# Chunk attention and a feed-forward block on one core: q and k loaded as one 4 KB run per partition

## The chip, the cores and the metric

The kernel runs on one core of a Trainium2 chip. The metric is the device time in microseconds (us) of one execution. Three runs of the kernel before took 244.71, 244.99 and 245.13 us; the median is 244.99. A separate, profiled execution gives the trace that the numbers of this text come from.

The core has engines that run side by side: TensorE (PE, matmuls; its weight loads are listed as PEld), VectorE (DVE), ScalarE (ACT), GpSimd (POOL) and SyncE (SP). They share 16 DMA engines. A tile in on-chip memory has 128 partitions; "partitions x elements" says how much an instruction works on.

## The reference

There are 8 batches, 8 heads, 576 tokens and 64 elements per head. Attention is local: each chunk of 64 tokens attends to itself alone. The result, with the heads side by side, is the input of a feed-forward block without a nonlinearity.

```
scores = scale * matmul(q_c, k_c transposed)          # 64 x 64 per chunk and head
attn   = exp(scores - max) / (sum + 1e-9)
x      = matmul(attn, v_c), as 4608 tokens x 512
a, b   = x @ w1, x @ w2                               # 512 -> 1024
out    = ((a * b) @ w3) @ w_out                       # 1024 -> 1024 -> 512
```

All inputs and the output are float32. The kernel computes in bf16 with float32 sums.

## The kernel before, in words

**Blocks.** The 4608 tokens are 72 chunks, four to a block: p = 0 to 17 counts blocks of 256 tokens, and a group g is two blocks. 576 tokens are nine chunks, so six of the blocks (2, 4, 6, 11, 13, 15) reach over the end of a batch; `spans` (line 118) cuts their loads in two.

**The order is written out by hand.** The string ORDER at the head of the file is a list of steps such as `T3.0`: a letter for a function and its arguments. Each engine gets its instructions in the order of the string, and `inorder` keeps it. So a late instruction makes everything late that stands behind it on its engine. The steps that the prediction speaks of:

- `R0`, `R1` (line 134): load block 0 of q and of k as float32, on SP's queue and on ACT's. `K0`, `K1` (line 140): ACT casts them to bf16.
- `q`, `k` (line 148): load a later block of q or k on POOL's queue, which casts to bf16 under way. POOL issues all weight and v loads on the same queue, in the order of the string.
- `T p.s` (line 202): DVE transposes q (s = 0) or k (s = 1) of block p, tile qk to tile qkT. DVE's transpose works on squares of 32 partitions by 32 elements, in the order in which it reads.
- `G` (line 212), only for blocks from 8 on: SP moves qkT to qkm, a form with 64 partitions, by DMAs (line 200).
- `S` (line 221): PE computes the scores of a block, from qkT for the blocks up to 7 (two products over 32 elements), from qkm after that (one over 64).
- `E` (line 238): ACT takes the exponential. `P` (line 245): PE multiplies with v and, by a column of ones in the v tile, sums the rows. `N` (line 265): DVE takes the reciprocal and normalises. `X` (line 279): DVE transposes to the tile xt, for the later blocks by way of xm and moves (`H`).
- `A`, `B` (lines 328, 332): PE multiplies with w1 and w2, `C` (line 335): ACT copies the first, `M` (line 339): DVE multiplies the two to the tile ab. For groups 0 and 1 this is done per block, with 256 columns, later per group with 512.
- `V`, `W`, `Z` (lines 391 to 406): w3 and w_out are multiplied together once, on the chip. DVE transposes w3 (tile w3T, line 393), PE multiplies.
- `O`, `Y`, `Q` (lines 363 to 387): PE multiplies ab with that product, ACT copies, SP stores.
- `D` (line 304): multiplications of zeros. They fill PE's time ahead of the first steps, in a fixed number.

PSUM, where PE writes, has four tiles, which S, P, A with B, W and O take in turn (`psum`). A branch at the end (`do_rescue`) computes everything again in a safer way if a check of the sums fails; it isn't entered with these inputs, but it calls the same `load_qk` and `do_T`.

**Where q and k lie.** In a quadrant of 32 partitions there is one chunk. Before the change a partition holds two neighbouring tokens (t) of all eight heads (h): eight runs of 2 x 64 float32, 512 B each, are read from memory for it, and eight of 256 B are written as bf16. Partition y of the quadrant has tokens 2y and 2y + 1. The transpose reads a partition's 1024 elements in the order in which they lie: h, t, half of the head's 64 elements (e), 32 elements. It turns "32 partitions y by 32 elements" into "32 partitions by 32 values of y". In qkT a head has its 64 tokens side by side (`[P, 2, 2, 2, H, CH]`, the last index is the token), so the 32 values of y are written two elements apart.

Of the kernel before, what the change touches and what calls it, by code (L numbers as in the profile page):

```python
# [44 lines left out]
def kernel(  # L45
# [11 lines left out]
    nc = tc.nc  # L57
    B, H, S, D = q.shape
    P = 128
    BL = 32  # L60
    NB = P // BL
    CH = 64
# [14 lines left out]
    bf = mybir.dt.bfloat16  # L77
    f32 = mybir.dt.float32
# [4 lines left out]
    io = ctx.enter_context(tc.tile_pool(name="io", bufs=2))  # L83
    asb = ctx.enter_context(tc.tile_pool(name="asb", bufs=2))
    msb = ctx.enter_context(tc.tile_pool(name="msb", bufs=2))
    ps = ctx.enter_context(tc.tile_pool(name="ps", bufs=4, space=bass.MemoryType.PSUM))

    def inorder(ins):
        tc.keep_in_program_order(ins)
        return ins  # L90
# [4 lines left out]
    def load(dst, src):  # L95
        return inorder(nc.gpsimd.dma_start(dst, src))  # L96
# [21 lines left out]
    def spans(c0, n):  # L118

        at = 0  # L120
        while at < n:
            b, c = divmod(c0 + at, NCH)
            m = min(n - at, NCH - c)
            yield at, b, c, m
            at += m
# [2 lines left out]

    qk_t = {}

    HH = H // 2
    raw_t = {}

    def do_R(s):

        raw_t[s] = msb.tile([P, H, 2 * D], f32, tag="o_sb", name="raw")
        inorder((nc.sync, nc.scalar)[s].dma_start(
            raw_t[s][:], (q, k)[s][0, :, 0:4 * CH, :].rearrange("h (p t) d -> p h (t d)", t=2)))

    def do_K(s):  # L140
        if 0 not in qk_t:
            qk_t[0] = io.tile([P, 2, H, 2 * D], bf, tag="qk", bufs=5, name="qk")
        inorder(nc.scalar.copy(qk_t[0][:, s], raw_t[s][:]))  # L143

    def heads(h):
        return slice(0, H) if h is None else slice(h * HH, (h + 1) * HH)

    def load_qk(p, which, h=None):
        if p not in qk_t:
            qk_t[p] = io.tile([P, 2, H, 2 * D], bf, tag="qk", bufs=5, name="qk")  # L150
        for s in which:
            for at, b, c, m in spans(4 * p, 4):
                load(qk_t[p][at * BL:(at + m) * BL, s, heads(h)],
                     (q, k)[s][b, heads(h), c * CH:(c + m) * CH, :].rearrange("h (p t) d -> p h (t d)", t=2))

    def do_w(p):

# [36 lines left out]
    qkT_t, qkm_t, s_t, e_t, pv_t, xn_t, xm_t, xt_t = {}, {}, {}, {}, {}, {}, {}, {}  # L194
# [4 lines left out]
    def move(dst, src):  # L199
        inorder(nc.sync.dma_start(dst, src))  # L200

    def do_T(p, s, h=None):


        g = p // 2
        if g not in qkT_t:
            qkT_t[g] = asb.tile([P, 2, 2, 2, H, CH], bf, tag="qkT", bufs=2, name="qkT")
        inorder(nc.vector.transpose(  # L208
            qkT_t[g][:, :, p % 2, s, heads(h)].rearrange("p e h (y t) -> p h t e y", t=2),
            qk_t[p][:, s, heads(h)].rearrange("p h (t e y) -> p h t e y", t=2, e=2)))  # L210

    def do_G(g, a):

# [218 lines left out]
    def do_rescue():  # L432
# [8 lines left out]
        for g in range((NP + 1) // 2):  # L441
            for p in (2 * g, 2 * g + 1):
                load_qk(p, (0, 1))
                load_v(p)
                do_T(p, 0)
                do_T(p, 1)
                s_ps = psum("s_ps")
                for h in range(H):
# [36 lines left out]
            t.clear()  # L485
            t.update(was)

    def load_q(p, h=None):
        load_qk(p, (0,), h)

    def load_k(p, h=None):
        load_qk(p, (1,), h)

    def load_w12(i):
        n = DF // 4
# [3 lines left out]
    def load_half3(i):  # L499
# [8 lines left out]


    do = {"q": load_q, "k": load_k, "v": load_v, "i": load_w12, "o": load_wo, "h": load_half3, "T": do_T, "S": do_S, "R": do_R, "K": do_K, "E": do_E, "w": do_w, "x": do_x, "G": do_G, "H": do_H,  # L510
          "P": do_P, "N": do_N, "X": do_X, "A": do_A, "B": do_B, "C": do_C, "M": do_M, "D": do_D, "V": do_V,
          "W": do_W, "Z": do_Z, "O": do_O, "Y": do_Y, "Q": do_Q, "F": do_F, "L": do_L}
# [40 lines left out]
```

## Time and profile before

| what | value |
|---|---|
| median of three runs | 244.99 us |
| the profiled execution | 245.28 us |
| its span, first to last instruction | 243.5 us |
| granted TensorE clock | 1.00 |
| 36 transposes of q and k (line 208), DVE | 45.1 us busy, 1289 ns each |
| loads of q and of k on POOL | 23 and 23 issues, 791 and 786 ns each |
| a load of 256 KB of q, of k, issue to landing (median) | 7.2 us, 7.8 us |
| R0, R1, issue to landing | 5.4 us, 6.3 us |
| packets of POOL's queue (q0) | 82592, 18.88 MB |

How to read it: the span and the busy times come from the profiled execution. Around the span lie 1.8 us that belong to the execution's time. The page of the profile lists each engine's busy time, then the span in 40 equal slices with one digit for the busy tenth of each, then queues, a chain of work followed back from the end, and groups of instructions: line, engine, operation, what is written from what, shape and count; busy time and the mean of one in ns; the idle time before them and what ended it. The view of waits has lines "engine and line <- what it waited for: us in total, times, longest". The view of windows has for each stretch its length, the busy time of engines, the granted clock, the DMA engines' share (above 1 where packets overlap) and GB/s.

### The profile page before, as it was taken

How to read it: one execution, taken by the hardware profiler on the slowest of the kernel's cores; microseconds unless marked ns; L12 is line 12 of the kernel's file. 1: busy time of each engine (PE TensorE's matmuls, PEld its weight loads, DVE VectorE, ACT ScalarE, POOL GpSimd, SP SyncE). 2: the span in 40 equal slices, each digit the busy share in tenths (PEclk: the TensorE clock that was granted, in tenths of full speed). 3: DMA queues.
4: the chain of work that ended last, by engine and by line, in shares of the span. 5: the costliest groups of instructions: out<-in, count | busy, mean ns of one | idle time of the engine just before them, and what ended most of it. 6: DMA issues, size and time to landing. Idle time of an engine off the chain costs nothing.

```text
span 243.5 us, 6405 instructions
## 1 busy us (share of the span) xinstructions
PE 227.4 (93%) x2753; PEld 120.3 (49%) x2753; DVE 155.3 (64%) x238; ACT 85.2 (35%) x116; POOL 83.3 (34%) x112
## 2 busy tenths in 40 slices
PE   1299989999999999999999999999999999999994
PEld 1147878864545444444444444444444444444442
DVE  1756799699799588999998899918451332143000
ACT  2412323423333334425326335162332332322322
POOL 8847875555985344753260140000000000000000
PEclk9999999999999999999999999999999999999999
DMA  7999999999999999999999793735502200400244
GB/s 177 179 185 180 185 168 201 196 193 170 164 174 218 228 216 259 182 215 198 213 214 242 213 134 95 164 78 213 145 0 92 86 0 0 173 2 1 90 174 172
DMA packets 93744, 37.68 MB, mean 155 GB/s; under 512 B 75152, under 2 KB 86672, under 8 KB 93712
## 3 DMA queue, kind: packets, MB, share of 16 engines
q0 software_dynamic: 82592, 18.88, 83.7%
q1 hardware_dynamic: 10080, 17.83, 24.1%
q10 hardware_dynamic: 1040, 0.52, 0.8%
q8 instruction: 22, 0.36, 0.6%
q14 instruction: 10, 0.08, 0.1%
HBM read 38.80 MB, written 9.44 MB: 198 GB/s over the span
## 4 chain that ended last, share of the span: by engine, by line
PE 76%; DMA 14%; DVE 3%; POOL 2%; SPq 1%; issue 1%; ACT 0%; DVEq 0%; POOLq 0%
PE ab_ps L93 40%; PE o_ps L93 26%; PE w_ps L93 6%; DMA w<-in_moe_w_dram 4%; DMA qkm<-qkT 4%; DMA qk<-in_k_dram 3%; DMA qk<-in_q_dram 3%; PE s_ps L93 3%; PE pv L93 3%; DVE qkT L208 2%; SPq L200 1%; POOL vbuf L96 1%; POOL w L96 1%; DVE xt L283 1%; DVE xn L271 1%
## 5 line engine op out<-in xcount | busy, mean ns | idle before, releaser
L93 PE MATMUL ab_ps<-xt,w 128*128 128x512 bf16 (+1 forms) x688 | 127.2, 342 | 0.7 <-DVE xt L283 0.6
L93 PEld LDWEIGHTS <-w 128*128 128x128 bf16 x704 | 67.0, 98 | 55.5 <-issue 1.2
L352 DVE TENSOR_TENSOR ab<-a_sb,ab_ps 128x512 bf16<-128x512 f32 x71 | 47.6, 674 | 40.8 <-ACT a_sb L337 40.6
L337 ACT COPY a_sb<-ab_ps 128x512 f32<-128x512 f32 x71 | 41.6, 586 | 81.3 <-PE ab_ps L93 81.1
L93 PE MATMUL o_ps<-w3o,ab 128*128 128x512 bf16 (+1 forms) x296 | 63.9, 373 | 0.0
L208 DVE STREAM_TRANSPOSE qkT<-qk 128x1024 bf16<-128x1024 bf16 x36 | 45.1, 1289 | 7.3 <-ACT qk L143 5.6
L93 PEld LDWEIGHTS <-ab 128*128 128x128 bf16 x296 | 28.4, 98 | 32.3
L96 POOL DMA_DIRECT2D vbuf<-in_v_dram x40 | 33.9, 857 | 19.2 <-DMA qk<-in_k_dram 6.3
L382 ACT COPY o_sb<-o_ps 128x1024 f32<-128x1024 f32 x17 | 17.2, 1012 | 45.2 <-PE o_ps L93 41.3
L271 DVE TENSOR_TENSOR xn<-pv,rcs 128x512 bf16<-128x512 f32 x36 | 24.9, 692 | 1.4
L96 POOL DMA_DIRECT2D qk<-in_q_dram x23 | 18.2, 791 | 9.4 <-DVE ab L352 2.0
L96 POOL DMA_DIRECT2D qk<-in_k_dram x23 | 18.0, 786 | 7.2 <-DMA vbuf<-in_v_dram 4.9
L241 ACT ACTIVATE e<-s_ps 128x1024 bf16<-128x1024 f32 x16 | 15.9, 1027 | 2.5 <-PE s_ps L93 2.2
L93 PE MATMUL w_ps<-wo,w3T 128*128 128x512 bf16 x64 | 14.0, 379 | 0.0
L291 DVE STREAM_TRANSPOSE xm<-xn 128x512 bf16<-128x512 bf16 x20 | 13.6, 697 | 0.2
L268 DVE RECIPROCAL rcs<-pv 128x8 f32<-128x8 f32 x36 | 6.9, 192 | 10.3 <-PE pv L93 10.3
L96 POOL DMA_DIRECT2D w<-in_moe_w_dram x16 | 11.1, 697 | 5.4 <-DMA wo<-in_moe_w_out_dram 2.8
L93 PEld LDWEIGHTS <-e 64*32 64x32 bf16 (+1 forms) x832 | 7.8, 97 | 8.7 <-issue 6.9
L93 PE MATMUL pv<-vbuf,e 64*32 64x65 bf16 (+1 forms) x832 | 10.2, 198 | 1.8 <-ACT e L241 1.1
L283 DVE STREAM_TRANSPOSE xt<-xn 128x512 bf16<-128x512 bf16 x16 | 11.4, 711 | 0.5
L375 DVE COPY o_sb<-o_ps 128x256 f32<-128x256 f32 x1 | 0.4, 425 | 16.1 <-PE o_ps L93 16.1
L93 PEld LDWEIGHTS <-qkT 32*64 32x64 bf16 x512 | 5.6, 117 | 10.3 <-DVE qkT L208 8.0
(30 smaller groups left out, 55.6 us busy)
## 6 DMA issues: line engine op xcount, KB each, us to landing
out_dram<-o_sb SPq DMA_DIRECT2D x17, 512.0 KB, 4.0
qkm<-qkT SPq DMA_DIRECT2D x40, 128.0 KB, 5.2
vbuf<-in_v_dram POOLq DMA_DIRECT2D x32, 128.0 KB, 8.4
w<-in_moe_w_dram POOLq DMA_DIRECT2D x16, 256.0 KB, 9.9
qk<-in_q_dram POOLq DMA_DIRECT2D x11, 256.0 KB, 7.2
qk<-in_k_dram POOLq DMA_DIRECT2D x11, 256.0 KB, 7.8
xt<-xm SPq DMA_DIRECT2D x40, 64.0 KB, 3.3
wo<-in_moe_w_out_dram POOLq DMA_DIRECT2D x4, 256.0 KB, 6.8
```

What stands on the lines that cost most here:

```text
L93: return inorder(nc.tensor.matmul(*a, **kw))
L96: return inorder(nc.gpsimd.dma_start(dst, src))
L200: inorder(nc.sync.dma_start(dst, src))
L208: inorder(nc.vector.transpose(qkT_t[g][:, :, p % 2, s, heads(h)].rearrange("p e h (y t) -> p h t e y", t=2), qk_t[p][:, s, heads(h)].rearr ...
L241: inorder(nc.scalar.activation(e_t[p][:, :, heads(hh)], s_t[p][:].rearrange("p u (h q) -> p u h q", q=CH)[:, :, heads(hh)], Exp, scale=sca ...
L268: inorder(nc.vector.reciprocal(rc, pv[:, :, :, D:W]))
L271: inorder(nc.vector.tensor_mul(xn_t[p][:, u], pv[:, :, :, 0:D], rc.to_broadcast([P, 2, 4, D])))
L283: inorder(nc.vector.transpose(new_xt(g)[:].rearrange("p (o t) -> p o t", o=KO)[:, :, t0:t0 + UT] .rearrange("p o (m y) -> p m o y", y=BL), ...
L291: inorder(nc.vector.transpose(xm_t[g][:, u, :, m].rearrange("p o (c y) -> p c o y", y=BL), xn_t[p][:].rearrange("p u r m d -> p (u r) m d" ...
L337: inorder(nc.scalar.copy(a_t[p, j][:], ps_t[p, j][:, 0, :]))
L352: inorder(nc.vector.tensor_mul(o, view(a_t.pop((p, j))[:]), view(ps_t.pop((p, j))[:, 1, :])))
L382: inorder(nc.scalar.copy(o_sb[:], ps_t.pop(p)[:]))
```

## The change

A partition now holds sixteen neighbouring tokens of one head: one run of 16 x 64 float32, 4 KB, written as 2 KB of bf16. The quadrant of a chunk has four groups of sixteen tokens (g) by eight heads, so partition 8g + h. The first loads (R), the later loads (q, k) and the transposes change; the tile qkT and all that reads it stay as they are, and ORDER stays as it is. The argument that chose half of the heads, which ORDER doesn't use for these steps, goes.

```diff
+    RT = CH * H // BL
+
+    def runs(ap, b, c, m):
+
+        return ap[b, :, c * CH:(c + m) * CH, :].rearrange("h (g t) d -> g h (t d)", t=RT)
...
-        raw_t[s] = msb.tile([P, H, 2 * D], f32, tag="o_sb", name="raw")
-        inorder((nc.sync, nc.scalar)[s].dma_start(
-            raw_t[s][:], (q, k)[s][0, :, 0:4 * CH, :].rearrange("h (p t) d -> p h (t d)", t=2)))
+        raw_t[s] = msb.tile([P, RT * D], f32, tag="o_sb", name="raw")
+        inorder((nc.sync, nc.scalar)[s].dma_start(raw_t[s][:], runs((q, k)[s], 0, 0, 4)))
...
-    def load_qk(p, which, h=None):
+    def load_qk(p, which):
         if p not in qk_t:
-            qk_t[p] = io.tile([P, 2, H, 2 * D], bf, tag="qk", bufs=5, name="qk")
+            qk_t[p] = io.tile([P, 2, RT * D], bf, tag="qk", bufs=5, name="qk")
         for s in which:
             for at, b, c, m in spans(4 * p, 4):
-                load(qk_t[p][at * BL:(at + m) * BL, s, heads(h)],
-                     (q, k)[s][b, heads(h), c * CH:(c + m) * CH, :].rearrange("h (p t) d -> p h (t d)", t=2))
+                load(qk_t[p][at * BL:(at + m) * BL, s, :], runs((q, k)[s], b, c, m))
...
-    def do_T(p, s, h=None):
-
-
+    def do_T(p, s):
         g = p // 2
...
         inorder(nc.vector.transpose(
-            qkT_t[g][:, :, p % 2, s, heads(h)].rearrange("p e h (y t) -> p h t e y", t=2),
-            qk_t[p][:, s, heads(h)].rearrange("p h (t e y) -> p h t e y", t=2, e=2)))
+            qkT_t[g][:, :, p % 2, s].rearrange("p e h (b t) -> p t e b h", t=RT),
+            qk_t[p][:, s].rearrange("p (t e b h) -> p t e b h", t=RT, e=2, h=H)))
```

In the new transpose the 1024 elements of a partition are still read in the order in which they lie. A square now has "32 partitions (four groups b, eight heads h) by 32 elements", and its 32 values are written with b sixteen elements apart and h, the inner index, a whole head's 64 tokens apart.

## The prediction

> **What bounds the kernel now.** I read the busy totals first, then the slices, then who waited for whom.
>
> ```profile
> PE 227.4 (93%) x2753; PEld 120.3 (49%) x2753; DVE 155.3 (64%) x238; ACT 85.2 (35%) x116; POOL 83.3 (34%) x112
> ...
> PE   1299989999999999999999999999999999999994
> ...
> DVE  1756799699799588999998899918451332143000
> ...
> DMA  7999999999999999999999793735502200400244
> ```
>
> PE works nearly without a break from the third slice (6.1 us each) to the last. VectorE (DVE) and the DMA engines are both near full up to slice 25, so they are the engines on which a price can come out, while a gain can only come from PE's idle time. That idle time is in PE's waits:
>
> ```profile
> PE z_ps L93 <- DVE qkT L208: 7.4, 1, 7.4
> ...
> PE ab_ps L93 <- DVE xt L283: 0.6, 2, 0.3
> PE s_ps L93 <- DMA qkm<-qkT: 0.4, 1, 0.4
> ```
>
> One wait of 7.4 us stands at the start: the first scores need T0.0 and T0.1. Everything later is tenths. In the windows from 12.2 to 160 us PE's busy times fall short of the window lengths by 2.9 us in all. So after the start at most some 3 us can be won, whatever becomes faster.
>
> Next, which slack DVE has. The view of windows, cut by stage, for all of DVE:
>
> ```profile
> 12.20:30.40 18.20, 11.89 (x20) 1.00 1.75 184
> 30.40:60.00 29.60, 26.44 (x35) 1.00 1.69 186
> 60.00:80.00 20.00, 18.06 (x23) 1.00 1.93 190
> 80.00:97.00 17.00, 12.58 (x22) 1.00 1.57 231
> 97.00:113.50 16.50, 15.39 (x25) 1.00 1.80 197
> 113.50:131.00 17.50, 16.34 (x24) 1.00 1.49 209
> 131.00:148.00 17.00, 15.07 (x24) 1.00 1.16 189
> ```
>
> The columns are window, length, DVE busy (instructions), clock, DMA share, GB/s. DVE's idle time is 6.3, 3.2, 1.9, 4.4, 1.1, 1.2 and 1.9 us, 20.0 us in all. By the timeline the 36 q/k transposes lie as 4 (before 12.5), 2, 4, 10 (60 to 80), 4 (T10 and T11, to 99.4), 2, 6 and 4, the last one ending at 148.8.
>
> **The change part by part.**
>
> *The loads through POOL's queue (34 full-size loads' worth).* Before, one q or k load is 1024 runs of 512 B read and 256 B written; after, 128 runs of 4 KB read and 2 KB written. The page's share of packet time (83.7% for q0) suggests a large saving, but packets overlap (the windows' DMA share is above 1), so I price by throughput, in stretches where by the issue order one kind of load alone is under way:
>
> ```profile
> 33.00:35.00 2.00, 2.00 (x21) 1.76 (x18) 1.90 (x5) 0.59 (x1) 1.58 (x3) 1.00 1.83 178
> 38.00:41.00 3.00, 3.00 (x96) 2.47 (x89) 3.00 (x4) 1.65 (x3) 1.79 (x3) 1.00 1.24 205
> 44.00:46.00 2.00, 2.00 (x78) 1.71 (x77) 1.66 (x3) 1.61 (x2) 1.46 (x2) 1.00 1.44 194
> ```
>
> The last number is GB/s, counted as written. Runs of 256 B (q, k) go at 178, of 512 B (weights) at 194, of 1 KB (the wo weights) at 205. A 262 KB load takes 262/178 = 1.47 us, and at 205 it takes 1.28: 0.19 us less, x34 = 6.6 us of the DMA stream. Bounds: nothing, or somewhat more than 0.19 if 2 KB runs go above the 205 row; I take 0.19, by the longest run that the trace has. It is beside PE's work: after the start PE's waits name one DMA, a move, with 0.4 us. POOL's issue falls too (786 ns for 1024 runs; 581 ns is the row with fewest), at most 0.2 x 46 = 9 us of an engine that is 34% busy. Gain on the path: 0 to 1 us.
>
> The Trainium skill ("DMA: Bandwidth & Descriptors", Why small descriptors are slow) gives a 256-byte descriptor 27% overhead; by it, as an estimate, a load would fall to 1.16 us and the stream by 10.6 us. The rows' 13% (178 against 205) is the smaller figure, and either is hidden.
>
> *The two first loads (R0, R1).* 1.05 MB on the queues of SP and ACT, landed 5.4 and 6.3 us after issue, at 6.14 and 7.11; the window 3 to 5 us shows 319 GB/s. At the rate at which the 1 KB weight loads read (2 x 205 = 410 GB/s, since they read f32 and write bf16) 1.05 MB takes 2.6 us instead of 3.3. Little arrives before 3 us, and fewer runs may also mean an earlier first byte. Bounds: nothing, and 1.8 us (the first load alone at 410 from about 2 us, with the landing's own delay). I take **1.0 us**. It is on the path: cast K0 (1.04 us), T0.0, T0.1, S0 follow at once. What is late next: E0, P0 and five fixed batches of zero matmuls, which keep the shift to A0.0.
>
> *The casts, matmuls, moves.* K reads and writes the same 1024 contiguous elements; qkT keeps its layout, so S, G and everything behind it keep their cost: nothing, both ways. Loads that cross a batch boundary (12 of the 34 pairs of tensor and block) remain two DMAs; their outermost source step now counts 4 to 12 groups, and if these spread over fewer engines, a 64 KB load is slower by about a microsecond, in a stream that PE hardly waits for: nothing.
>
> *The transposes: the step that decides.* Each T still reads 1024 contiguous elements; its write changes. Before, neighbours in the stream land 2 elements (4 B) apart; after, 64 elements (128 B) apart. No transpose of the trace writes so. The rows around it:
>
> ```profile
> L208 DVE STREAM_TRANSPOSE qkT<-qk 128x1024 bf16<-128x1024 bf16 x36 | 45.1, 1289 | 7.3 <-ACT qk L143 5.6 <-DMA qk<-in_q_dram 1.3
> L393 DVE STREAM_TRANSPOSE w3T<-w 128x1024 bf16<-128x1024 bf16 x8 | 9.4, 1217 | 1.2 <-DMA w<-in_moe_w_dram 1.2
> L113 DVE MEMSET zero<- 128x256 uint32 x1 | 0.3, 272 | 0.9 <-PEq L537 0.9
> L116 DVE MEMSET vbuf<- 128x16 bf16 x6 | 0.4, 72 | 0.0
> ```
>
> - Lower end: no price. w3T writes side by side (2 B) and takes 1217, qkT with 4 B steps 1289. If the 72 ns are all that not being neighbours costs, the new form stays at 1289. Below 1217, its own kind's contiguous row, nothing speaks for it.
> - 72 ns more for one doubling of the step, repeated for the five doublings from 4 to 128 B, is +360 ns.
> - Upper end: the memset of vbuf's ones writes 16 elements 160 B apart in 72 ns, at most 4.5 ns each; the contiguous memset does 272/256 = 1.06. A transpose's element costs (1217 - 697)/512 = 1.02 ns, from w3T (1024 elements) and xm (512); with 4.5 in its place a transpose takes 3.5 us more.
>
> By its step the memset is the nearest row, but its 72 ns hold a fixed part that the trace doesn't separate. I take the smallest whole step inside its bound: a second 1.02 ns for each element that has no neighbour, **+1.04 us** a transpose.
>
> The Trainium skill ("Advanced Engine Details and Errata", SBUF Cachelines) speaks against the change: accesses that each fall in a different 16-byte line are penalised, and two hits a line are needed to hide the latency. No run here shows it; the 4 B step has four elements a line, the new step one. The page has no time; read as two steps an element, an estimate, it would make about the same.
>
> *The sum, with +1.04.* Lag of DVE, and of PE where nothing leads:
> - Start: T0.0 and T0.1 are on the path, +2.1 - 1.0. T1.0 and T1.1 stand ahead of N0.0 on DVE, so X0.1 ends 4.2 - 1.0 = 3.2 later; the zero matmuls (X0.1 ends at 15.7, A0.0 starts at 17.0) take 1.2 of it. PE +2.0.
> - T2: S2 starts at 27.73, straight after T2.1. PE +4.1.
> - 30 to 60: 4 x 1.04 = 4.2 against 3.2 idle, S3 straight after T3.1; the 13.8 us of w_ps matmuls absorb the rest. About +4.8.
> - 60 to 80: 10 x 1.04 = 10.4 against 1.9. DVE +13.3; behind T5 to T9 wait N, X and M, for which A, B and the PSUM buffers wait.
> - 80 to 99: T10, T11, +4.2 against 4.4. T11's moves land at 113.4 and S10 starts at 113.5: no lead. PE +13.1.
> - 99 to 149: 12 x 1.04 = 12.5 against 4.2. DVE +21.4; S16 (158.8) has about 1 us of lead over the last moves. PE +20.4. Then only PE bounds, and nothing comes back.
>
> A second way: 36 x 1.04 = 37.4, less all 20.0 idle, less 1.0, is 16.4, which assumes that all idle time absorbs; the stages show where it can't. I take +20. The profiled execution is 245.3 (span 243.5 and 1.8 around it), 0.3 above the median of 245.0. 245.3 + 20 - 0.3 = **265**.
>
> **The rivals.**
> 1. *The step is free* (ends on the other side). T stays at 1289; R lands 1.0 earlier and the tighter stream takes up to 1 of PE's 2.9 us. For it: qkT against w3T, only 6% for a step twice as wide. Against: the memset leaves room for 4 times the price. Time 245.0 - 1.5 = 243.5 (242 to 244.8; if the runs don't speed the loads, 245). It holds while the price is under about 0.1 us: T0.0 and T0.1 then eat no more than 0.2 of the 1.0.
> 2. *A middle price*, +0.36. DVE +13, mostly in idle time: start +0.7 - 1.0; T5 to T9 +3.6 against 1.9, then 4.4 idle; T11 +0.7 with no lead; 12 x 0.36 = 4.3 against 4.2. I add 2.5: 247.5 (245.5 to 253).
> 3. *The memset's whole price*, +3.5: 36 x 3.5 = 126, less 20: 350.
>
> **How the numbers follow.** Forecast 0.40 (its own range 257 to 272), free step 0.35, middle 0.19, memset's price 0.06. The range over all: from 242 to 272 only the tails and the dear case are left out. 0.2%, 0.5 us, is about what a measurement of this kernel can tell from no change. Faster 0.32 (the free step but for its edge), same 0.04 (that edge and the middle's), slower 0.64.
>
> **What would show it.** L208's mean: near 2330 (forecast), 1290 (rival 1), 1650 (rival 2), above 4000 (rival 3). R landing near 5.1 instead of 6.1. q0's packets from 82592 to about 52000. With the forecast, DVE near 193 us busy, its slices full to the 25th and beyond, new PE waits on qkT, xt and ab, and s_ps behind qkm's moves. Wrong if L208 stays and PE still loses time, or if L208 grows and the idle time of DVE swallows it.

## The result, and the profile after

The changed kernel takes **362.47 us** (median of 4 runs, 360.4 to 362.87), the kernel before 245.06 us (median of 4): ratio 1.4776, 95% interval 1.4716 to 1.4836. The prediction was 265 us, with a range up to 272. So the sign was right, the size far off, and the rival that came closest was the third one (350 us), which had a chance of 0.06.

The page of the changed kernel, its busy totals and slices (one slice is now 9.0 us):

```profile
PE 258.6 (72%) x2753; PEld 129.9 (36%) x2753; DVE 275.1 (76%) x238; ACT 85.5 (24%) x116; POOL 74.1 (21%) x112
...
PE   1159485599847547555796594359579999999996
...
DVE  3995999978999999989799999996974742322300
...
PEclk9999969889996959969696679588969999999999
DMA  9999999980094906976670198228251521103034
```

Up to slice 30 the full row is now DVE's, and PE's has the holes. The DMA row has holes as well: POOL holds its loads back until DVE and PE have emptied the buffers. DVE is busy 119.8 us longer than before (275.1 against 155.3), and one group carries all of it. The rows of that group, of w3T, whose code did not change, and of the loads:

```profile
L210 DVE STREAM_TRANSPOSE qkT<-qk 128x1024 bf16<-128x1024 bf16 x36 | 167.0, 4801 | 5.1 <-ACT qk L148 5.1
L395 DVE STREAM_TRANSPOSE w3T<-w 128x1024 bf16<-128x1024 bf16 x8 | 9.7, 1230 | 0.9 <-PE w_ps L93 0.9
L96 POOL DMA_DIRECT2D qk<-in_q_dram x23 | 13.2, 575 | 45.8 <-DVE qkT L210 34.9
```

A transpose of q or k takes 4801 ns instead of 1289; w3T stays at 1230. POOL's queue stood idle for 9.4 us in all ahead of its loads of q before; now it is 45.8 us, and 34.9 of them end with a transpose, which frees the load's buffer.

What PE waits for, from the view of waits (us in total, times, longest):

```profile
PE ab_ps L93 <- DVE ab L354: 31.8, 6, 7.2
PE o_ps L93 <- DVE xn L273: 15.9, 3, 9.9
PE z_ps L93 <- DVE qkT L210: 13.7, 1, 13.7
PE s_ps L93 <- DVE qkT L210: 12.9, 3, 6.7
```

Only 26.6 us of these are waits for a transpose itself. The larger part is waits for ab and xn, short work of DVE that stands in its queue behind a transpose: the hand-written order makes everything late that is behind a slow instruction.

### The profile page after: what moved, and what is told of

Its sections match the earlier page's. It is cut to its first block, busy times and chain, and to the rows that moved or that the text cites. A ratio compares the mean times of both kernels' runs of the same rounds, so it can differ in the third digit from the quotient of the medians.

```text
span 361.0 us, 6405 instructions
## 1 busy us (share of the span) xinstructions
PE 258.6 (72%) x2753; PEld 129.9 (36%) x2753; DVE 275.1 (76%) x238; ACT 85.5 (24%) x116; POOL 74.1 (21%) x112
## 3 DMA queue, kind: packets, MB, share of 16 engines
q0 software_dynamic: 53664, 18.89, 46.1%
## 4 chain that ended last, share of the span: by engine, by line
DVE 40%; PE 37%; DMA 14%; issue 4%; POOL 2%; SPq 1%; ACT 0%; DVEq 0%; POOLq 0%
DVE qkT L210 33%; PE ab_ps L93 23%; PE o_ps L93 12%; DMA w<-in_moe_w_dram 5%; DMA qk<-in_k_dram 5%; DVE ab L354 3%; DMA qk<-in_q_dram 3%; PE w_ps L93 2%; DVE xn L273 1%; SPq L204 1%; DMA vbuf<-in_v_dram 1%; DVE xt L285 1%; POOL vbuf L96 1%; DVE xm L293 1%; POOL wo L96 1%
## 5 line engine op out<-in xcount | busy, mean ns | idle before, releaser
L210 DVE STREAM_TRANSPOSE qkT<-qk 128x1024 bf16<-128x1024 bf16 x36 | 167.0, 4801 | 5.1 <-ACT qk L148 5.1
L93 PE MATMUL ab_ps<-xt,w 128*128 128x512 bf16 (+1 forms) x688 | 144.0, 371 | 33.8 <-DVE ab L354 31.8
L93 PEld LDWEIGHTS <-w 128*128 128x128 bf16 x704 | 72.8, 106 | 99.5 <-issue 47.3
L354 DVE TENSOR_TENSOR ab<-a_sb,ab_ps 128x512 bf16<-128x512 f32 x71 | 51.0, 725 | 45.6 <-ACT a_sb L339 45.5
L93 PE MATMUL o_ps<-w3o,ab 128*128 128x512 bf16 (+1 forms) x296 | 74.4, 415 | 15.9 <-DVE xn L273 15.9
L93 PEld LDWEIGHTS <-ab 128*128 128x128 bf16 x296 | 30.7, 106 | 56.5 <-DVE xn L273 17.0
L96 POOL DMA_DIRECT2D qk<-in_q_dram x23 | 13.2, 575 | 45.8 <-DVE qkT L210 34.9
L93 PE MATMUL s_ps<-qkT 32*64 32x64 bf16 x384 | 4.7, 202 | 14.8 <-DVE qkT L210 12.9
L93 PE MATMUL z_ps<-qkT 32*64 32x64 bf16 x128 | 2.1, 237 | 18.0 <-DVE qkT L210 13.7
L96 POOL DMA_DIRECT2D qk<-in_k_dram x23 | 12.7, 556 | 3.1 <-DMA w<-in_moe_w_dram 2.6
```

The costliest lines, as they stand in the source:

```text
L93: return inorder(nc.tensor.matmul(*a, **kw))
L210: inorder(nc.vector.transpose(qkT_t[g][:, :, p % 2, s].rearrange("p e h (b t) -> p t e b h", t=RT), qk_t[p][:, s].rearrange("p (t e b h) - ...
L354: inorder(nc.vector.tensor_mul(o, view(a_t.pop((p, j))[:]), view(ps_t.pop((p, j))[:, 1, :])))
```

## The experiments

Two theories were put against each other first: all of the loss is the wider step of the transposes' writes; or part of it comes from the loads, whose buffers and landings shift.

**The two halves of the change, each alone.** The first kernel has the new loads, and transposes that still write 4 B apart (so the scores are of other pairs of tokens; the work is the same):

```diff
-            qkT_t[g][:, :, p % 2, s].rearrange("p e h (b t) -> p t e b h", t=RT),
-            qk_t[p][:, s].rearrange("p (t e b h) -> p t e b h", t=RT, e=2, h=H)))
+            qkT_t[g][:, :, p % 2, s].rearrange("p e h (y t) -> p h t e y", t=2),
+            qk_t[p][:, s].rearrange("p (h t e y) -> p h t e y", t=2, e=2, h=H)))
```

> The changed kernel's loads with the transposes of before: they read the same 1024 contiguous elements and write neighbours 4 B apart again. The heads and tokens of the scores are mixed up by this, so the attention is of other pairs than the reference's; the amount of work is the same. Theory W (the write step of the transposes is the whole of the loss): a transpose near 1290 ns, 243 to 245 us, a little under the 245.06 of before, since R0 landed 0.5 us earlier in the changed kernel. Rival L (the loads cost time as well: the second first load landed 0.9 us later in the changed kernel, and loads that are cut at a batch's end had more small packets): a transpose near 1290 ns and yet 246 to 255 us, with PE waiting for q or k.

Measured: 244.53 us, ratio to before 0.9988 (0.9959 to 1.0017). The row of its transposes, and of PE's first wait:

```profile
L210 DVE STREAM_TRANSPOSE qkT<-qk 128x1024 bf16<-128x1024 bf16 x36 | 45.0, 1288 | 7.8 <-ACT qk L148 6.6
```
```profile
PE z_ps L93 <- DVE qkT L210: 8.6, 1, 8.6
```

The second kernel has the loads of before, and transposes that write 128 B apart (again the scores are of other pairs):

```diff
-            qkT_t[g][:, :, p % 2, s, heads(h)].rearrange("p e h (y t) -> p h t e y", t=2),
-            qk_t[p][:, s, heads(h)].rearrange("p h (t e y) -> p h t e y", t=2, e=2)))
+            qkT_t[g][:, :, p % 2, s].rearrange("p e h (b t) -> p t e b h", t=16),
+            qk_t[p][:, s].rearrange("p h x -> p (h x)").rearrange("p (t e b h) -> p t e b h", t=16, e=2, h=H)))
```

> The kernel before with only the transposes' writes of the changed kernel (64 elements apart); loads as before. Here too the scores are of other pairs of tokens and heads than the reference's, with the same work. Theory W: transposes near 4800 ns and 361 to 365 us, the changed kernel's 362.5 or a little more. Rival L: clearly less than 362, by what the loads cost; under 355 if they cost more than 7 us.

Measured: 361.97 us, ratio 1.476 (1.4675 to 1.4845).

```profile
L208 DVE STREAM_TRANSPOSE qkT<-qk 128x1024 bf16<-128x1024 bf16 x36 | 166.8, 4798 | 5.6 <-ACT qk L143 5.6
```

So the transposes' writes alone make the whole loss, and the loads alone make no difference that can be told. Within the kernel with the new loads there are two small things of opposite sign. The first scores start 1.2 us later than before (10.93 against 9.75), since k's first load lands later. By S16 PE has won that back (158.06 against 158.83). Of these 2.0 us, 1.7 are three pauses of PE in the trace of before that this trace doesn't have: 0.66 and 0.59 us in which PE waited for nothing that the profile shows, and 0.44 us for moves to qkm. That the later loads are the reason is not shown.

**What a write step costs, by itself.** A kernel without any of the computation runs rows of one kind of instruction on zeros: transposes, copies and memsets whose neighbours are written, or read, a chosen distance apart. The core of it:

```diff
+    for s in (1, 2, 4, 8, 16, 32, 64, 66, 128):
+        t = tile_of(f"tw{s}x", s)
+        for _ in range(N):
+            inorder(nc.vector.transpose(spread(t, s), flat(src, s)))
...
+    for s in (1, 2, 4, 8, 16, 64):
+        t = tile_of(f"cw{s}x", s)
+        for _ in range(N):
+            inorder(nc.vector.tensor_copy(spread(t, s), flat(src, s)))
...
+    t = pool.tile([P, 256, 80], bf, name="memx")
+    for n in (16, 64, 256):
+        for _ in range(N):
+            inorder(nc.vector.memset(t[:, 0:n, 0:1], 1.0))
```

> None of the reference's computation: only rows of VectorE and ScalarE instructions on 128 x 1024 bf16, six of each form, one after the other, and zeros stored as output. Transposes that write neighbours 2, 4, 8, 16, 32, 64, 128, 132 and 256 B apart; the two forms of the kernels; forms with half of the heads or with eight heads side by side; transposes that read apart; copies that write or read apart; memsets of 16, 64 and 256 elements 160 B apart. Theory W: the form of the changed kernel takes 4.5 to 4.8 us alone too, and the price sets in with the step: 2 to 8 B near 1.2 us, then up to about 4.5 us, at 128 B and 132 B alike; copies that write 128 B apart pay about the same per element, memsets too (256 elements near 1.1 us). Rival P (steps that are multiples of a power of two fall on the same place): 132 B near 1.2 us while 128 and 256 B take 4.5. Rival X (other engines' and DMAs' accesses make it slow): with all else idle the form of the changed kernel takes well under 4 us. Rival T (it belongs to the transpose): copies and memsets don't pay.

Its groups, from the view by line and shape. The number in a tile's name is the step in elements of 2 B; tw is a transpose's write step, tr its read step, cw a copy's write step on DVE, aw on ACT. The last two figures that matter are busy us and the mean of one in ns:

```profile
L57 DVE STREAM_TRANSPOSE tw1x<-src 128x1024 bf16<-128x1024 bf16 x6 | 7.4, 1236 | 0.2
L57 DVE STREAM_TRANSPOSE tw2x<-src 128x1024 bf16<-128x1024 bf16 x6 | 7.8, 1304 | 0.2
L57 DVE STREAM_TRANSPOSE tw4x<-src 128x1024 bf16<-128x1024 bf16 x6 | 14.6, 2436 | 0.2
L57 DVE STREAM_TRANSPOSE tw8x<-src 128x1024 bf16<-128x1024 bf16 x6 | 28.4, 4734 | 0.2
L57 DVE STREAM_TRANSPOSE tw64x<-src 128x1024 bf16<-128x1024 bf16 x6 | 28.6, 4761 | 0.2
L57 DVE STREAM_TRANSPOSE tw66x<-src 128x1024 bf16<-128x1024 bf16 x6 | 28.3, 4710 | 0.2
L83 DVE STREAM_TRANSPOSE tr64x<-wide 128x1024 bf16<-128x1024 bf16 x6 | 11.3, 1884 | 0.2
L88 DVE COPY cw8x<-src 128x1024 bf16<-128x1024 bf16 x6 | 14.6, 2437 | 0.2
L97 ACT COPY aw8x<-src 128x1024 bf16<-128x1024 bf16 x6 | 28.4, 4732 | 0.2
L102 DVE MEMSET memx<- 128x256 bf16 x6 | 1.6, 272 | 5.5 <-DVE memx L102 5.5
L102 DVE MEMSET memx<- 128x16 bf16 x6 | 0.4, 72 | 0.6
```

The first six rows are one curve. From 2 to 4 B the step is almost free; at 8 B the time doubles, at 16 B it doubles again, and then it is flat to 256 B (4544 to 4761). One reading gives all of them: a transpose pays 1.02 ns an element, or about 4.6 ns each time its write goes on to another piece of 16 B, whichever is more. At 16 B and above, each of the 1024 elements goes on to another piece: 1024 x 4.6 = 4.7 us. At 8 B there are 512 such steps, 2.4 us. At 4 B there are 256, 1.2 us, which is just what the elements cost anyway. It is the order that counts: the tile of the 16 B row is written full, 128 pieces in all, and still every element pays. So the kernel before stood on the last step that is nearly free. An odd multiple of 4 B (tw66, 132 B) costs the same as 128 B, so it is not a matter of powers of two; and from 81 us on this kernel has nothing beside DVE's rows (its stores lie in the first 30 us, ACT's copies end at 80), so the price at 128 B and more is not a collision with other engines or with DMAs.

The price is not the transpose's own: from 16 B on an ACT copy pays the same (1044 ns side by side), a DVE copy about half of it (421 ns side by side, and already 730 at 4 B). Reads 128 B apart cost less than writes, 1884 against the 1236 of neighbours.

The last two rows concern the prediction's upper end. A memset of 256 strided elements is recorded with 272 ns, which is what the contiguous one in the prediction's rows takes too. One of 16 is recorded with 72 ns, so the record grows by only 0.83 ns an element, and some 59 of the 72 ns are a fixed part. The price stands in the other column: each of the following memsets of 256 waits 0.92 us for the one before, so one comes every 1.19 us, 4.65 ns an element. By this the recorded duration ends before the writes do. The 72 ns of vbuf's memset, 4.5 ns an element, hit the right figure by luck: the recorded time was no measure of the writes.

**A price in the middle.** Does the stage sum itself work? The loads of before, with transposes that write 8 B apart, cost about what the forecast had assumed (the scores are again of other pairs):

```diff
-            qkT_t[g][:, :, p % 2, s, heads(h)].rearrange("p e h (y t) -> p h t e y", t=2),
-            qk_t[p][:, s, heads(h)].rearrange("p h (t e y) -> p h t e y", t=2, e=2)))
+            qkT_t[g][:, :, p % 2, s].rearrange("p e h c -> p e (h c)").rearrange("p e (a j t) -> p a t e j", a=4, t=4),
+            qk_t[p][:, s].rearrange("p h x -> p (h x)").rearrange("p (a t e j) -> p a t e j", a=4, t=4, e=2)))
```

> The kernel before, with the transposes writing neighbours 4 elements (8 B) apart; the scores are of other pairs of heads and tokens than the reference's, with the same work. Alone, such a transpose took 2436 ns against 1336: +1.1 us, nearly the +1.04 that the forecast assumed. So this run tests the second half of the forecast, what the kernel makes of such a price. If the sum by stages was right (+20 for +1.04): 264 to 270 us, with PE waiting for DVE and the last transposes some 20 us late. Rival A (the idle time of DVE takes most of it): under 255. Rival B (each longer wait of PE lowers the granted clock, and PE's work after it becomes longer too): above 272, the clock under 0.97.

Measured: 272.02 us, ratio 1.1118 (1.1073 to 1.1162), granted clock 0.987.

```profile
L208 DVE STREAM_TRANSPOSE qkT<-qk 128x1024 bf16<-128x1024 bf16 x36 | 85.2, 2450 | 5.7 <-ACT qk L143 5.7
```

The price is +1.16 us a transpose, and the span grows by 26.3 us. The time is 2 us above the expected range. The forecast's stages, with 1.16 in place of 1.04 and without the 1.0 us for the first loads, come to about 25. The lag also builds up where the forecast had it: the scores start 6.8 us later than before at S5, 13.5 at S8 and 25.8 at S16, where the forecast, with its smaller price, had 4.8, 13.1 and 20.4. So the way from the price to the time was sound to a microsecond or two. The rival with the lower clock expected a clock under 0.97, and the four runs have 0.975 to 0.987: a slower PE can be only a small part here.

**The layout turned the other way.** If DVE should not write apart, PE can read apart. The tile qkT has the heads innermost; the transposes of the new loads then write eight heads side by side, and PE reads 16 B apart:

```diff
-            qkT_t[g] = asb.tile([P, 2, 2, 2, H, CH], bf, tag="qkT", bufs=2, name="qkT")
+            qkT_t[g] = asb.tile([P, 2, 2, 2, CH, H], bf, tag="qkT", bufs=2, name="qkT")
...
-            qkT_t[g][:, :, p % 2, s].rearrange("p e h (b t) -> p t e b h", t=RT),
+            qkT_t[g][:, :, p % 2, s].rearrange("p e (b t) h -> p t e b h", t=RT),
...
-                           lhsT=qkT_t[g][blk[i], e, m, 1, h, :], rhs=qkT_t[g][blk[i], e, m, 0, h, :],
+                           lhsT=qkT_t[g][blk[i], e, m, 1, :, h], rhs=qkT_t[g][blk[i], e, m, 0, :, h],
```

> The changed kernel's loads, and qkT with the eight heads of a token side by side: the transposes write runs of 8 elements (16 B), and PE reads a head's 64 tokens 16 B apart, as weights and as the moving operand. Theory W: a transpose 1.2 to 1.6 us, the loss is gone but for what PE pays; 832 score matmuls with 64 columns each and their weight loads: if PE reads 16 B steps at full rate 243 to 246 us, if at half rate some 10 ns more on each of the 832 pairs, 8 us, 250 to 254 us. Rival (any write that isn't side by side pays, however dense): transposes above 2 us and more than 270 us.

Measured: 261.82 us, ratio 1.0694 (1.0638 to 1.075), granted clock 1.0.

```profile
L210 DVE STREAM_TRANSPOSE qkT<-qk 128x1024 bf16<-128x1024 bf16 x36 | 42.8, 1218 | 7.6 <-ACT qk L148 6.4
L93 PE MATMUL s_ps<-qkT 32*64 32x64 bf16 x384 | 13.0, 298 | 0.0
```

DVE's loss is gone: 1218 ns, less than before. PE pays instead. In the kernel with the new loads alone these 384 matmuls are 4.2 us busy; by the timeline a batch of 64 weight loads and matmuls takes 2.17 us instead of 0.71, so 34 ns a pair instead of 11. With 832 such matmuls that is some 19 us, and PE's busy time is 242.8 us against 224.8. PE is the bound, so nearly all of it shows: 17.3 us more than with the new loads alone. The expectation allowed at most 254 us, with 10 ns more for a pair; it was 23.

The last step in that direction splits the heads into two groups of four: each T becomes two transposes of 512 elements that write four heads side by side (8 B), and PE reads 8 B apart:

```diff
-            qkT_t[g] = asb.tile([P, 2, 2, 2, H, CH], bf, tag="qkT", bufs=2, name="qkT")
+            qkT_t[g] = asb.tile([P, 2, 2, 2, 2, CH, 4], bf, tag="qkT", bufs=2, name="qkT")
...
+        for e in range(2):
+            inorder(nc.vector.transpose(
+                qkT_t[g][:, e, p % 2, s].rearrange("p f (b t) r -> p t b f r", t=RT),
+                qk_t[p][:, s].rearrange("p (t e b f r) -> p e t b f r", t=RT, e=2, f=2, r=4)[:, e]))
...
+                           lhsT=qkT_t[g][blk[i], e, m, 1, h // 4, :, h % 4], rhs=qkT_t[g][blk[i], e, m, 0, h // 4, :, h % 4],
```

> The changed kernel's loads, and qkT with four heads of a token side by side (8 B): the transposes, cut into two for each block, write runs of four elements; PE reads a head's tokens 8 B apart. If DVE pays by the 16 B of SBUF that a run touches, 4.4 ns each time, four elements a visit cost 1.1 ns each, just what the transpose takes anyway: two halves of about 0.7 us. If PE reads 8 B steps at full rate: 244 to 247 us, a few tenths over the loads alone for the doubled number of transposes. If PE pays here as at 16 B (34 ns for a pair of weight load and matmul, not 10): about 262 as there; if it pays half of that, 250 to 254.

Measured: 248.87 us, ratio 1.0166 (1.0144 to 1.0189).

```profile
L211 DVE STREAM_TRANSPOSE qkT<-qk 128x512 bf16<-128x512 bf16 x72 | 44.9, 677 | 6.9 <-ACT qk L148 6.3 <-DMA qk<-in_q_dram 0.6
L93 PE MATMUL s_ps<-qkT 32*64 32x64 bf16 x384 | 7.0, 229 | 0.0
```

A transpose of 512 takes 677 ns, no more than the contiguous xm (697 in the kernel before): four neighbours to a piece are free, as the curve says. PE's pairs take 18 ns each, and its busy time is 230.3 us. The time lies between the branches of the expectation: 8 B steps are neither free for PE nor half as dear as 16 B.

**The first loads.** Why does k's first load land later with 4 KB runs? One idea was that the two loads compete and the second queue loses; so each was cut in two halves of 2 KB runs, one half on each queue (added to the kernel with the new loads alone):

```diff
-        inorder((nc.sync, nc.scalar)[s].dma_start(raw_t[s][:], runs((q, k)[s], 0, 0, 4)))
+        n = RT * D // 2
+        for i, queue in enumerate((nc.sync, nc.scalar)):
+            inorder(queue.dma_start(raw_t[s][:, i * n:(i + 1) * n], runs((q, k)[s], 0, 0, 4)[:, :, i * n:(i + 1) * n]))
```

> The loads of the changed kernel with cheap transposes once more (the scores of other pairs, as in the run with the loads alone), and each of the two first loads cut into two halves of 2 KB runs, one on SP's queue and one on ACT's. In the run with the loads alone the second first load landed at 8.0 us, 0.9 later than before, and PE's first scores began 1.2 us later. Theory: that lateness eats what the other loads win; with both landed by 7 us the scores start 1 to 2 us sooner and the time is 242.5 to 243.8. Rival: the start isn't what bounds (w loads and PE's row of work behind are), and 244.3 to 244.8 stays.

Measured: 245.04 us against 245.0, ratio 1.0001 (0.9988 to 1.0013). The second cast still starts at 8.4 us and the first scores at 10.87. So this cut wins nothing. It doesn't rule out that the queues compete, for both halves of k stand behind a half of q.

The traces show where the time goes, though not why. Counted from their packets, q's data begin at 1.9 us and k's at 3.2 before, but at 2.3 and 4.3 in the kernel with the new loads alone: k's load runs mostly after q's, no longer beside it. And while it runs the rate is lower: the windows from 4 to 5 and from 5 to 6 us show 340 and 276 GB/s before, 234 and 238 with the new loads alone. POOL's loads are not what takes the rate, since their first packet there starts at 6.6 us. Why long runs start k's load so late, and move less per microsecond, stays open.

No version beats the kernel before by more than the measurement can tell; the new loads alone (0.9988) are level with it.

## Why the prediction was wrong in size

**The step that failed** is the price of a transpose: "I take the smallest whole step inside its bound: a second 1.02 ns for each element that has no neighbour, +1.04 us". It measured +3.51 us (4801 against 1289). The upper end, +3.5, was the price, though by luck, as the memsets show. The text itself called its row the nearest by step, and set it aside because the 72 ns "hold a fixed part that the trace doesn't separate". That was a fair doubt about the row, but it was no ground for the value put in its place, which came from no row at all. The doublings row (+360 ns) fell as well: the curve has no even price for a doubling, it is flat up to 4 B, steep to 16 B and flat again.

**The way from price to time** held at the middle price, as the 8 B kernel shows, and came out short at the full price. The third rival took 36 x 3.5 = 126 and let 20 us of DVE's idle time absorb it: +106. Measured is +117.5 on the span. The same stretch of DVE's work, from the start to the end of the last q/k transpose, in the kernel before, in the one with 8 B steps and in the changed one (length, DVE busy, clock, DMA share, GB/s):

```profile
0.00:148.85 148.85, 122.10 (x179) 1.00 1.60 194
```
```profile
0.00:174.90 174.90, 159.88 (x179) 0.98 1.36 166
```
```profile
0.00:263.80 263.80, 241.88 (x179) 0.86 0.78 111
```

Length less busy is DVE's idle time in that stretch: 26.8, 15.0 and 21.9 us. The busy time grew by 119.8 rather than 126, because neighbours in DVE's queue overlap a little (the transposes themselves are busy 167.0 us for 36 x 4.80 = 172.8). But idle time absorbed 11.7 us at the middle price and only 4.8 at the full one. So 119.8 - 4.8 = 115 us, and 2.6 more after that stretch. Against the third rival's +106: idle time absorbed 15.2 us less than its 20, the busy time grew by some 6 less than its 126, and 2.6 came after the stretch. DVE idles more although it is the bound, because it in turn waits for PE, through ACT's copies behind PE's A matmuls. DVE's waits of that kind within these stretches, at 8 B and in the changed kernel (us in total, times, longest):

```profile
DVE ab L352 <- ACT a_sb L337: 5.5, 6, 2.7
```
```profile
DVE ab L354 <- ACT a_sb L339: 13.2, 11, 4.1
```

And PE is often slow when it comes back from a long stall. Windows over PE's matmuls in the changed kernel: 16 of ab_ps after a wait of 7.24 us, then 8 after no wait (PE, PEld, DVE, ACT and POOL busy, then the clock):

```profile
157.14:162.48 5.34, 5.34 (x17) 1.90 (x16) 3.96 (x8) 0.59 (x1) 0.00 (x0) 0.66 0.24 45
163.12:164.95 1.83, 1.83 (x16) 0.70 (x8) 1.75 (x2) 1.83 (x3) 0.00 (x0) 1.00 0.00 0
```

The granted clock is 0.66 in the first window and 1.00 in the second; 16 matmuls take 5.34 us, where two batches of 8 without a wait make 3.7. Behind the six waits of ab_ps on ab, of 3.0 to 7.2 us, the matmuls take 1.5 to 2.8 us longer than such a batch without a wait, 11 us in all, so this is of the right size. Not every stall has this price: after one of 2.99 us, before S5, the next 16 matmuls take the usual 3.6 us. That the lower clock is the whole of the missing absorption is argued from these windows; no run took the stalls away without changing the transposes.

**The other steps.**
- *Loads through POOL's queue*: 205 GB/s for the long runs was right (about 100 packets of 2 KB land per us when they are alone), the packets were 53664 against "about 52000", and POOL's issue is 575 ns against the 581 taken. That nothing of it shows in the time was right too: level, by the kernel with the loads alone. The estimate beside it, by the Trainium skill ("DMA: Bandwidth & Descriptors", Why small descriptors are slow), divides 1.47 us by 1.27; on the page the 27% are a share of the whole, so as an estimate it would be 1.47 x 0.73 = 1.07 us a load. At the 205 GB/s measured a load takes 1.28.
- *First loads, -1.0 us*: wrong in sign on the path. q's landed 0.5 us after issue earlier (4.9 against 5.4), but k's later, 7.2 against 6.3 (7.7 in the kernel with the loads alone), and the first scores need both. In the kernel with the loads alone this cost 1.2 us at the start.
- *Casts, matmuls, moves at nothing*: right. The casts take 1044 ns as before; the 64 KB pieces of loads that cross a batch's end land no later (q's 9.6 us after issue with the new loads alone, 11.1 before); PE's longer busy time (258.6 against 227.4) goes with the lower clock.
- *What would show it*: L208 "above 4000" for the third rival was the sign that appeared (the line is L210 now). Of the new PE waits that it named, those on qkT and ab came. Those on xt hardly grew (0.9 us against 0.6), and none stands behind qkm's moves; 15.9 us and more on xn, which it hadn't named, came instead.

The Trainium skill ("Advanced Engine Details and Errata", SBUF Cachelines) has the rule that the curve follows: accesses that each fall into another 16-byte line are penalised. The curve agrees on the 16 B, since nothing changes beyond that step. It differs on the rule that two hits a line hide the latency: with two elements a line (8 B) a transpose already takes 2436 ns against 1236; four are needed (4 B, 1304).

## What to carry to other kernels

Before you widen a write on the chip to get longer runs from memory, count how often the write, in its own order, goes on to another piece of 16 B: here each time cost about 4.6 ns in DVE's transposes and ACT's copies. So a transpose's bf16 steps of 4 B were nearly free, and steps of 16 B or more cost nearly four times, on an engine that was 64% busy. Turning the step over to PE's reads is not free either (11, 18 and 34 ns a pair at 2, 8 and 16 B). And where the nearest row gives a dear bound that can't be trusted, run that one instruction alone before pricing with it; a milder figure that no row shows is a wish.

## What the runs showed of the hardware that was not expected

- A strided memset's recorded duration (272 ns for 256 elements) seems to leave out most of its writes; the wait of the next memset on that tile shows them (1.19 us from one to the next).
- A transpose's reads are free at 8 B (1239 ns against 1236) and cost half as much again at 128 B (1884), while its writes cost nearly four times (4761).
- Larger runs do not make a first load land sooner in every queue: with 4 KB runs instead of 512 B, q's on SP's queue landed up to 0.5 us earlier and k's on ACT's queue 0.9 to 1.4 us later, its data beginning at 4.3 us instead of 3.2.
